# A linear state space layer and an H3 convolution on one core: finer PSUM items, a block of B by another queue, and a new order of the items

## The chip, the cores and the metric

One core of a Trainium2 chip. The metric is device microseconds of one execution of the whole program, as the median of several runs; lower is better.

## The reference

Two layers over 2,048 positions of 640 channels, side by side in the output. The first ("S5") has a diagonal complex state of 640; the second ("H3") gates a 4-tap convolution and convolves the result with a filter as long as the sequence, channel by channel.

```python
def _A_ref(x, Lambda_re, Lambda_im, B_re, B_im, C_re, C_im, log_dt, Dskip):
    Lam_bar = jnp.exp(dt * Lam)                      # 640 complex, dt = exp(log_dt)
    B_bar = ((Lam_bar - 1.0) / Lam)[:, None] * Bmat  # 640 x 640
    Bu = jnp.einsum("bld,pd->blp", x + 0j, B_bar)
    for t in range(L):
        h = Lam_bar[None, :] * h + Bu[:, t, :]
    y = 2.0 * jnp.einsum("blp,dp->bld", hseq, Cmat).real + x * Dskip

def _B_ref(q, k, v, shift_k, ssm_k, ssm_D):
    k_shift = sum of 4 shifted k, weighted by shift_k, per channel
    kv = k_shift * v
    y = causal convolution of kv with ssm_k (2,048 long), per channel, by FFT
    y = y + kv * ssm_D
    return q * y
return jnp.concatenate([a, b], axis=-1)              # 1 x 2048 x 1280, bf16
```

## The kernel before, in words

**S5.** Time is split in eight phases c, t = 8m + c, with m up to 256, so that the recurrence runs over m with the eighth power of Lam_bar. The phases of x are loaded transposed by SP's queue (`load_x`, L417, items `x0` to `x7`, two phases to a tile `xT`), and so is B (`turn_B`, L159): `B0` is the first block of 128 states, `B1` and `B3` two blocks each, and each item is one transpose for the real and one for the imaginary part. For each block j of 128 states, the PE items are `u1j` and `u3j` (B times the phases 1 and 5, 3 and 7, 512 columns for each of the real and the imaginary part, L434), `vj` (phases 2 and 6, joined with u1 by a diagonal matrix of powers of lambda, `diagL`, L449 and L450), `wj` (phase 4, joined with v and u3, 256 columns, L442) and `zj` (phase 0, joined with the seven others). Each is evicted to `u` in bf16 by an item with an e (`ue1j`, `vej`, `wej`, `zej`; L142 on ScalarE, L144 on VectorE). Then on VectorE `rsj` rotates z by a table of phases and scans it (L463 to L472), `roj` rotates back, and the states of the other phases are made from it: a product by a power of lambda (`m4j`, `m2j`, `m1j`, `m3j`; L306 on ScalarE, L308 on VectorE) and two additions (`r..`, L496). Last, sixteen items `p0` to `p15` project 128 rows each to 640 outputs, in two halves of 320 (L508). For thirteen of them the product of x and Dskip is loaded and made in rows (`xl`, `xm` L537) and added on VectorE as PSUM is read (`ye`, `dve_yx`, L523); for the other three it is five matmuls (L515) and a plain eviction. `yd` stores the rows.

**H3.** Channels go in five groups G of 128. `kT` and `vT` are loaded transposed (L561), `ks` copies k with its halves swapped, `dS` makes the diagonal matrices of the taps (L582), `tap` does the four taps on PE in 64x64 tiles (L594), `kv` multiplies by v out of PSUM (L599). `kvo` and `kvs` write kv to DRAM and read it back in another layout, `hs` loads the filter in that layout (L572), `had` adds ssm_D to it (L578). The long convolution is a two-stage transform on PE: `s1h` and `s1k` (L613), evicted to `As`; `s2` (L631), evicted to `XH`; the products `y` on VectorE (L645 to L648); the inverse `inv` (L659), evicted to `zz` (`zs`), two DMA transposes (`zt`, L667), the last stage `fin` (L681), and `ob`, which multiplies by q out of PSUM (L686). `qi` and `od` load q and store the output.

**Opening.** The tables of phases and the transform matrices are made in the kernel. Four short vectors (log_dt, Lambda_im, Lambda_re, Dskip) are loaded as rows by ScalarE's queue (`lv`, L147), PE turns them (`pv`, L247), ScalarE takes the exponent (`exp`, L250) and sine and cosine, and VectorE makes `lam` (L285), from which all powers of lambda come. `WARM` items (`wm`) are matmuls on a unit matrix ahead of S5's first products.

**Order.** `make_plan` gives each item its engine, cost, inputs and function; a planner outside of the kernel wrote the string `ORDER` from it, and the kernel issues the items in just that order, so each engine works through its items in the order of the string. `name@2` is the PSUM slot that the item uses, a trailing `v` puts an item that may run on either engine on VectorE (else ScalarE), `a` and `b` are the two buffers for the products m. PSUM is four tiles of two banks, `ps`, slots 0, 2, 4 and 6: each item of PE takes a whole tile, also `w` and `z`, which fill two half banks.

Of the kernel before, what the change touches and what calls it, by code (L numbers as in the profile page):

```python
# [46 lines left out]
class Kernel:  # L47


    def __init__(self, ctx, tc, out, ins):  # L50
# [95 lines left out]
    def load_vec(self, eng, v, ap):  # L146
        eng.dma_start(out=self.vrow[v * NT:v * NT + NT, :], in_=ap.rearrange("(j i) -> j i", i=128))  # L147

# [266 lines left out]

    def load_x(self, c):
        self.nc.sync.dma_start_transpose(  # L417
            out=self.xc(c), in_=self.x2.rearrange("(m p) (k d) -> p m k d", p=T, d=128)[c])
# [10 lines left out]
    def pe_u(self, j, c, joins, ps):  # L429
        mm = self.nc.tensor.matmul  # L430
        x = self.__dict__[f"xT{c}"]
        for r in range(2):
            for k in range(NT):
                mm(ps[:, r, :], lhsT=self.BT[:, r, k, j * 128:(j + 1) * 128], rhs=x[:, :, k, :],  # L434
                   start=(k == 0), stop=(not joins and k == NT - 1))
        self.join(j, joins, ps, lambda c2, r: self.pair(j, c2, r), 2 * M)

    def pe_w(self, j, c, joins, ps):
        mm = self.nc.tensor.matmul
        for r in range(2):  # L440
            for k in range(NT):
                mm(ps[:, r, 0:M], lhsT=self.BT[:, r, k, j * 128:(j + 1) * 128], rhs=self.xc(c)[:, k, :], start=(k == 0), stop=False)  # L442
        self.join(j, joins, ps, lambda c2, r: self.u(j, c2, int(c2 > c))[:, r, :], M)

    def join(self, j, joins, ps, src, n):
        mm = self.nc.tensor.matmul
        for r in range(2):
            for i, (s, c2) in enumerate(joins):
                mm(ps[:, r, 0:n], lhsT=self.dl(j)[:, 3 * s, :], rhs=src(c2, r), start=False, stop=False)  # L449
                mm(ps[:, r, 0:n], lhsT=self.dl(j)[:, 3 * s + 2 - r, :], rhs=src(c2, 1 - r), start=False, stop=(i == len(joins) - 1))  # L450
# [47 lines left out]
    def pe_proj(self, c, i, skip, ps):  # L498
# [3 lines left out]
        for b in range(2):  # L502
            o = ps[:, b, :]
            c0 = 320 * b
            for j in range(NT):
                h = self.u(j, c)
                for r in range(2):
                    mm(o[:, 0:320], lhsT=h[:, r, ts], rhs=self.Cs[:, r, j, c0:c0 + 320], start=(j == 0 and r == 0),  # L508
                       stop=(skip and j == NT - 1 and r == 1))
            if skip:  # L510
                continue
            pieces = [(d, max(c0, d * 128), min(c0 + 320, d * 128 + 128)) for d in range(NT)]
            pieces = [q for q in pieces if q[1] < q[2]]
            for q, (d, lo, hi) in enumerate(pieces):
                mm(o[:, lo - c0:hi - c0], lhsT=xT[:, d, ts], rhs=self.diagD[:, d, lo - d * 128:hi - d * 128],  # L515
                   start=False, stop=(q == len(pieces) - 1))

    def ev_y(self, eng, n, ps):
        out = self.yo[:, n % NYO, :].rearrange("q (b n) -> q b n", b=2)
        self.copy(eng, out, ps[:, :, 0:320])  # L520

    def dve_yx(self, n, ps):
        self.nc.vector.tensor_tensor(out=self.yo[:, n % NYO, :].rearrange("q (b n) -> q b n", b=2), in0=ps[:, :, 0:320],  # L523
                                     in1=self.xr(n).rearrange("q (b n) -> q b n", b=2), op=ALU.add)
# [168 lines left out]
def make_plan(K):  # L693
# [87 lines left out]
    for c in (1, 5, 3, 7, 2, 6, 4, 0):  # L781
        dmat(f"x{c}", 1.4, 0.3275, (), lambda c=c: K.load_x(c))
    for j in range(NT):
        bt = [f"B{(j - 1) // 2 * 2 + 1 if j else 0}"]
# [5 lines left out]
        ev(f"ve{j}", 1024, [f"v{j}", "zer"], lambda eng, ps, j=j: K.ev_u(eng, j, 2, ps), f"v{j}")  # L790
        pe(f"w{j}", 18 * P256, 36, ["x4", f"dL{j}", f"ue3{j}", f"ve{j}"] + bt, lambda ps, j=j: K.pe_w(j, 4, ((0, 3), (1, 2)), ps), f"w{j}")
        ev(f"we{j}", 512, [f"w{j}", "zer"], lambda eng, ps, j=j: K.ev_half(eng, j, 4, ps), f"w{j}")
        pe(f"z{j}", 22 * P256, 44, ["x0", f"we{j}"] + bt, lambda ps, j=j: K.pe_w(j, 0, ((0, 7), (1, 6), (2, 4)), ps), f"z{j}")
        ev(f"ze{j}", 512, [f"z{j}"], lambda eng, ps, j=j: K.ev_half(eng, j, 0, ps), f"z{j}")
# [175 lines left out]
```

## Time and profile before

| | |
|---|---|
| median of 3 runs | 197.31 us (196.41 to 197.58) |
| the profiled execution | 196.7 us |
| its span in the profile | 194.8 us, 7,192 instructions |
| PE busy | 177.1 us (91%), 3,125 matmuls |
| VectorE busy | 171.5 us (88%), 355 instructions |
| ScalarE busy | 152.4 us (78%), 207 instructions |
| GpSimd busy | 19.4 us (10%), all in the opening |
| DMA | 34.87 MB, mean 179 GB/s |
| granted clock of PE | 1.00 throughout |

The span is the time from the first to the last instruction in the profile; 1.9 us of the execution lie around it. PE is TensorE's matmuls, PEld its weight loads, DVE VectorE, ACT ScalarE, POOL GpSimd, SP the engine that issues most DMAs; a name with q at its end (SPq, ACTq) is the time that an engine took to issue a DMA. L523 is line 523 of the kernel. A row of a timeline has the start and the length in us, the engine, the line, output and inputs with their sizes, the count, and in brackets how long the engine stood idle just before and on whom it waited. A row of a group has the busy time in us and the mean of one in ns, then the idle time before. A row on a DMA ends with the median time from issue to landing in us.

### The profile page before, as it was taken

Reading aid. Unit: us, or ns where it says so; the run is one execution under the profiler, and the core shown is the slowest. Engines: PE = TensorE matmul, PEld = TensorE weight load, DVE = VectorE, ACT = ScalarE, POOL = GpSimd, SP = SyncE. Lnnn points to the kernel's source line nnn. Section 1 sums busy time; section 2 is a strip of 40 time slices with the busy share of each in tenths; the row PEclk is TensorE's granted clock in tenths of the full one; section 3 lists DMA queues with packets and bytes.
Section 4 is the critical chain, followed back from the end, with each engine's and each line's share of the span. In section 5 each row is a group of like instructions: output and inputs, shape, how many; then the busy total and the mean of one; then the engine's idle time right before and its main releaser. Section 6 shows DMA issues by size and latency. Waiting matters only on the chain. (4 is left out here: it accounts for less than half of the span.)

```text
span 194.8 us, 7192 instructions
## 1 busy us (share of the span) xinstructions
PE 177.1 (91%) x3125; PEld 122.6 (63%) x3125; DVE 171.5 (88%) x355; ACT 152.4 (78%) x207; POOL 19.4 (10%) x46
## 2 busy tenths in 40 slices
PE   7779799698989998999999896899899999999992
PEld 2233366555567757644887785677678777778771
DVE  1495966998999999999999999999899999999593
ACT  3674959696899998999999899978996799790000
POOL 8599402000000000000000000000000000000000
PEclk9999999999999999999999999999999999999999
DMA  5999999999999999799679998797730996698926
GB/s 103 169 170 191 182 151 184 270 199 175 228 168 161 196 279 189 123 182 294 111 140 168 164 283 163 136 178 175 183 112 8 216 233 136 173 204 209 274 73 207
DMA packets 133022, 34.87 MB, mean 179 GB/s; under 512 B 128512, under 2 KB 132352, under 8 KB 132992
## 3 DMA queue, kind: packets, MB, share of 16 engines
q1 hardware_dynamic: 132952, 34.42, 89.9%
q8 instruction: 24, 0.39, 0.9%
q14 instruction: 6, 0.05, 0.1%
q10 hardware_dynamic: 40, 0.01, 0.0%
HBM read 10.17 MB, written 7.86 MB: 93 GB/s over the span
## 5 line engine op out<-in xcount | busy, mean ns | idle before, releaser
L508 PE MATMUL ps<-Cs,u 128*128 128x320 bf16 x320 | 45.6, 299 | 0.9 <-DVE yo L523 0.6
L142 ACT CAST As<-ps 128x1024 bf16<-128x1024 f32 x40 | 38.9, 1033 | 3.8 <-PE ps L613 2.3
L508 PEld LDWEIGHTS <-u 128*128 128x128 bf16 x320 | 30.5, 98 | 12.9 <-issue 0.9
L142 ACT CAST XH<-ps 128x1024 bf16<-128x1024 f32 x38 | 36.0, 1029 | 2.4 <-PE ps L631 2.1
L434 PE MATMUL ps<-xT,BT 128*128 128x512 bf16 x150 | 34.4, 379 | 3.2 <-DMA xT<-in_A_x_dram 1.1
L434 PEld LDWEIGHTS <-BT 128*128 128x128 bf16 x150 | 13.9, 98 | 20.4 <-DMA xT<-in_A_x_dram 1.6
L496 DVE TENSOR_TENSOR u<-tmp,u 128x1024 bf16<-128x1024 bf16 (+1 forms) x40 | 24.5, 622 | 1.0
L142 ACT CAST u<-ps 128x1024 bf16<-128x1024 f32 (+1 forms) x20 | 16.7, 835 | 6.7 <-PE ps L434 3.4
L142 ACT CAST zz<-ps 128x1024 bf16<-128x1024 f32 x19 | 18.8, 1034 | 3.1 <-PE ps L659 3.1
L631 PE MATMUL ps<-As,Gre 64*64 64x256 bf16 x320 | 19.6, 274 | 1.5 <-DVE vT L599 0.6
L631 PE MATMUL ps<-As,nGim 64*64 64x128 bf16 x320 | 18.4, 216 | 0.4 <-issue 0.4
L631 PE MATMUL ps<-As,Gim 64*64 64x128 bf16 x320 | 18.3, 216 | 0.0
L449 PE MATMUL ps<-u,diagL 128*128 128x256 bf16 (+1 forms) x60 | 15.3, 290 | 0.0
L450 PE MATMUL ps<-u,diagL 128*128 128x256 bf16 (+1 forms) x60 | 15.3, 291 | 0.0
L599 DVE TENSOR_TENSOR vT<-ps,vT 128x1024 bf16<-128x1024 f32 x10 | 11.9, 1217 | 2.6 <-PE ps L450 1.5
L631 PEld LDWEIGHTS <-Gre 64*64 64x64 bf16 x320 | 11.1, 106 | 4.9 <-issue 3.9
L306 ACT ACTIVATE tmp<-u,lam 128x512 bf16<-128x512 bf16 (+1 forms) x18 | 13.9, 868 | 0.0
L442 PE MATMUL ps<-xT,BT 128*128 128x256 bf16 x100 | 12.6, 273 | 1.1 <-DVE vT L599 0.9
L686 DVE TENSOR_TENSOR qb<-ps,qb 128x1024 bf16<-128x1024 f32 x10 | 12.0, 1215 | 1.5 <-DMA qb<-in_B_q_dram 1.5
L646 DVE TENSOR_TENSOR XH<-XH 128x2048 bf16<-128x2048 bf16 x10 | 12.2, 1225 | 0.5
L523 DVE TENSOR_TENSOR yo<-ps,BT 128x640 bf16<-128x640 f32 x13 | 10.7, 822 | 2.2 <-PE ps L508 0.9
L308 DVE TENSOR_SCALAR tmp<-u,lam 128x512 bf16<-128x512 bf16 (+2 forms) x42 | 12.5, 359 | 0.1
(161 smaller groups left out, 305.5 us busy)
## 6 DMA issues: line engine op xcount, KB each, us to landing
h_st<-in_B_ssm_k_dram SPq DMA_DIRECT2D x10, 256.0 KB, 4.6
kv_rows<-vT SPq DMA_DIRECT2D x5, 512.0 KB, 4.6
kv_st<-kv_rows SPq DMA_DIRECT2D x10, 256.0 KB, 5.2
qb<-in_B_q_dram SPq DMA_DIRECT2D x10, 256.0 KB
out_dram<-qb SPq DMA_DIRECT2D x10, 256.0 KB, 4.4
out_dram<-yo SPq DMA_DIRECT2D x16, 160.0 KB, 2.7
BT<-in_A_x_dram SPq DMA_DIRECT2D x13, 160.0 KB, 3.1
zz<-zz SPq DMA_TRANSPOSE x10, 4.7
```

Source lines behind the costliest of these rows:

```text
L142: self.nc.scalar.copy(out=out, in_=in_)
L306: self.nc.scalar.activation(out=out, in_=in_, func=ACT.Copy, scale=w)
L308: self.nc.vector.tensor_scalar_mul(out=out, in0=in_, scalar1=w)
L434: mm(ps[:, r, :], lhsT=self.BT[:, r, k, j * 128:(j + 1) * 128], rhs=x[:, :, k, :], start=(k == 0), stop=(not joins and k == NT - 1))
L442: mm(ps[:, r, 0:M], lhsT=self.BT[:, r, k, j * 128:(j + 1) * 128], rhs=self.xc(c)[:, k, :], start=(k == 0), stop=False)
L449: mm(ps[:, r, 0:n], lhsT=self.dl(j)[:, 3 * s, :], rhs=src(c2, r), start=False, stop=False)
L450: mm(ps[:, r, 0:n], lhsT=self.dl(j)[:, 3 * s + 2 - r, :], rhs=src(c2, 1 - r), start=False, stop=(i == len(joins) - 1))
L496: v.tensor_tensor(out=o, in0=buf[:, i, 0:n], in1=o, op=ALU.add)
L508: mm(o[:, 0:320], lhsT=h[:, r, ts], rhs=self.Cs[:, r, j, c0:c0 + 320], start=(j == 0 and r == 0), stop=(skip and j == NT - 1 and r == 1))
L631: mm(out, lhsT=w[rows, k, :], rhs=rhs, start=(w is self.Gre), stop=(w is self.Gim))
L646: tt(out=X, in0=X, in1=pl(0, 1).to_broadcast([128, 8, 2, 128]), op=ALU.mult)
L686: self.nc.vector.tensor_tensor(out=q, in0=ps[:].rearrange("p b (m e) -> p b m e", e=32), in1=q, op=ALU.mult)
```

## The change

Five things, in one edit:

1. **PSUM is one tile** of eight banks, `banks`. The four `ps` of H3 are now pairs of its banks. Items whose key begins with H, all of S5's, get a single bank (slots 0 to 7).
2. **S5's items are single banks.** `u1`, `u3` and `v` become two items each, one for the real and one for the imaginary part (`u10_0`, `u10_1`), with an eviction of 512 elements each in place of one of 1,024. `w` and `z` put both parts into one bank. A projection becomes two items, one for each half of 320 columns (`p0_0`, `p0_1`), and so do its skip addition or eviction.
3. **B's first block is loaded as it lies**, 128 rows of 640, by two loads on ScalarE's queue (`load_B`) into a part of `zz` that is free at that time, turned by ten matmuls on a unit matrix (`bt0_0`, `bt0_1`) and evicted into `BT` (`bte0_0`, `bte0_1`). The other four blocks stay transposed loads.
4. **The planner's rates for DMAs** differ a little, and hold a larger cost for `hs` and `kvs`.
5. **ORDER** is new throughout. (`JV` is empty, so the new branches on it and the class c = 6 aren't used.)

Matmuls, weights and transfers are otherwise the same.

```diff
 NPS = 4
+JB = 1
+JV = ()
...
-        self.ps = [psum.tile([128, 2, 512], f32, name=f"ps{i}") for i in range(NPS)]
+        self.banks = psum.tile([128, 8, 512], f32, name="banks")
+        self.ps = [self.banks[:, 2 * i:2 * i + 2, :] for i in range(NPS)]
...
+        self.Bn = self.zz[:, 0:2 * JB * D].rearrange("p (r j d) -> p r j d", r=2, j=JB)
...
+    def load_B(self, eng, j):
+        for r, ap in enumerate((self.A_B_re, self.A_B_im)):
+            eng.dma_start(out=self.Bn[:, r, j, :], in_=ap[128 * j:128 * j + 128, :])
...
+    def pe_bt(self, js, ks, ps):
+        mm = self.nc.tensor.matmul
+        i = 0
+        for j in js:
+            for k in ks:
+                re, im = (self.Bn[:, r, j, 128 * k:128 * k + 128] for r in range(2))
+                o_re, o_im = (ps[:, r, 128 * i:128 * i + 128] for r in range(2))
+                mm(o_re, lhsT=re, rhs=self.ident[:], start=True, stop=True)
+                mm(o_im, lhsT=im, rhs=self.ident[:], start=True, stop=True)
+                i += 1
...
-    def pe_u(self, j, c, joins, ps):
+    def pe_u(self, j, c, r, joins, ps):
+        x = self.__dict__[f"xT{c}"]
+        for k in range(NT):
+            self.nc.tensor.matmul(ps, lhsT=self.BT[:, r, k, j * 128:(j + 1) * 128], rhs=x[:, :, k, :],
+                                  start=(k == 0), stop=(not joins and k == NT - 1))
+        self.join(j, r, joins, ps, lambda c2, r: self.pair(j, c2, r))
...
+    def pe_w(self, j, c, joins, ps):
+        for r in range(2):
+            o = ps[:, M * r:M * r + M]
...
-    def dve_yx(self, n, ps):
-        self.nc.vector.tensor_tensor(out=self.yo[:, n % NYO, :].rearrange("q (b n) -> q b n", b=2), in0=ps[:, :, 0:320],
-                                     in1=self.xr(n).rearrange("q (b n) -> q b n", b=2), op=ALU.add)
+    def dve_yx(self, n, b, ps):
+        s = slice(320 * b, 320 * b + 320)
+        self.nc.vector.tensor_tensor(out=self.yo[:, n % NYO, s], in0=ps[:, 0:320], in1=self.xr(n)[:, s], op=ALU.add)
...
-    for j, n in ((0, 1), (1, 2), (3, 2)):
-        dmat(f"B{j}", 2.56 if n == 1 else 2.8, 0.3275 * n, (), lambda j=j, n=n: K.turn_B(j, n))
+    dma("B0", "ACT", 0.9, 0.36, ["lv"], lambda: K.load_B(nc.scalar, 0))
+    for j in (1, 3):
+        dmat(f"B{j}", 2.8, 0.655, (), lambda j=j: K.turn_B(j, 2))
...
-x1 x5 lv pc pc2 dc gp0 wm1@0 wt wm2@2 zer dc2 pp2 pp pv@4 exp@4 x7 B0 vec@4 rho Fi rr aM trig1 wm3@6 pc3 lam dL0@v x3 tp0 tab0
+zer x5 pc lv B0 pc3 zd x7 pc2 dc wm1@0 gp0 wm3@2 wt dc2 pp pv@4 exp@4 vec@4 dD wm2@6 rho Fi gp2 bt0_0@0 rr trig1 hk tp0 tab0
+bt0_1@2 bte0_1@2v wm0@4 hp0 x3 bte0_0@0v u30_1@0 dcol u30_0@1 gp1 gp3 x1 u10_0@2 lam dL0@v u10_1@3 u10e_1@3v tp1 dL1@v B1
```

SP's list in the opening, from its first transfer to the first group's k, v and filter. `xT` are phases of x, `BT` is B, `kT` is k, `dst` and `sk_b` the small vectors of H3. Before:

```order
L417 DMA_TRANSPOSE xT_133<-in_A_x_dram 128x5x256 x2
L417 DMA_TRANSPOSE xT_135<-in_A_x_dram 128x5x256
L159 DMA_TRANSPOSE BT<-in_A_B_re_dram 128x5x128
L159 DMA_TRANSPOSE BT<-in_A_B_im_dram 128x5x128
L417 DMA_TRANSPOSE xT_135<-in_A_x_dram 128x5x256
L159 DMA_TRANSPOSE BT<-in_A_B_re_dram 128x5x256
L159 DMA_TRANSPOSE BT<-in_A_B_im_dram 128x5x256
L417 DMA_TRANSPOSE xT_134<-in_A_x_dram 128x5x256
L162 DMA sk_b<-in_B_shift_k_dram 128x5x4
```

And now:

```order
L445 DMA_TRANSPOSE xT_130<-in_A_x_dram 128x5x256
L445 DMA_TRANSPOSE xT_132<-in_A_x_dram 128x5x256 x2
L570 DMA dst<-in_B_ssm_D_dram 2x5x64 x2
L445 DMA_TRANSPOSE xT_130<-in_A_x_dram 128x5x256
L167 DMA_TRANSPOSE BT<-in_A_B_re_dram 128x5x256
L167 DMA_TRANSPOSE BT<-in_A_B_im_dram 128x5x256
L445 DMA_TRANSPOSE xT_131<-in_A_x_dram 128x5x256 x2
L445 DMA_TRANSPOSE xT_129<-in_A_x_dram 128x5x256
L584 DMA_TRANSPOSE kT<-in_B_k_dram 128x2048
```

The two transposes of 128 states are gone, the two small loads of `dst` have come forward, and x's last phase, v and the filter h follow behind `kT` in both lists.

ScalarE's list up to the exponent and the first operations behind it, with the semaphores that each row waits for. `vrow` are the short vectors, `zz` the buffer that takes B's first block. Before:

```order
L147 DMA vrow<-in_A_Dskip_dram 5x128
L154 ACT_TABLE_LOAD
L154 ACTIVATE aph_88<-hpi 128x1 [waits DVE_49]
L250 ACTIVATE dt_b<-ps_66 128x5 [waits PE_49]
L275 ACTIVATE rr<-rho 128x5 [waits DVE_49]
```

And now:

```order
L151 DMA vrow<-in_A_Dskip_dram 5x128
L155 DMA zz<-in_A_B_re_dram 128x640
L155 DMA zz<-in_A_B_im_dram 128x640 [waits DMAHW0_49]
L162 ACT_TABLE_LOAD
L162 ACTIVATE aph_85<-hpi 128x1 [waits DVE_49]
L258 ACTIVATE dt_b<-banks 128x5 [waits PE_49]
L314 ACTIVATE diagD<-ident,vec 128x128 [waits DVE_49]
L314 ACTIVATE diagD<-ident,vec 128x128 x4
L283 ACTIVATE rr<-rho 128x5 [waits DVE_49]
```

Two issues stand ahead of the table load, the second of which waits for the DMA of log_dt, and the five `diagD` now stand ahead of `rr`.

VectorE's list just ahead of the first state scan (the row on `tab` is its first operation). `h_st` is the filter, `diagS` the taps' diagonals, `Mq` a matrix of the last stage, `kS` the swapped copy of k. Before:

```order
L578 TENSOR_TENSOR h_st<-h_st,dcol_b 128x32
L582 TENSOR_TENSOR diagS<-id_70,sk_b 128x512
L241 TENSOR_SCALAR m_cv<-m_cv 128x64
L242 TENSOR_TENSOR Mq<-m_cv,m_mask 128x256
L144 CAST u_138<-ps_64 128x2x2x256
L144 COPY kS<-kT 64x1032
L463 TENSOR_TENSOR tmp<-tab_123,u_137 128x512
```

And now:

```order
L148 CAST u_134<-banks 128x2x256
L622 TENSOR_TENSOR vT<-banks,vT 128x1024
L148 CAST u_135<-banks 128x2x256
L622 TENSOR_TENSOR vT<-banks,vT 128x1024
L249 TENSOR_SCALAR m_cv<-m_cv 128x64
L250 TENSOR_TENSOR Mq<-m_cv,m_mask 128x256
L605 TENSOR_TENSOR diagS<-id_67,sk_b 128x512
L601 TENSOR_TENSOR h_st<-h_st,dcol_b 128x32
L487 TENSOR_TENSOR tmp<-tab_120,u_134 128x512
```

The filter's operation now stands right ahead of the scan; an eviction and a copy of k that stood between them are elsewhere.

More of the change, by code (lines that the diff above doesn't have):

```diff
@@ L427, in pair @@
         return self.__dict__[f"u{j}"][:, c::4, r, 2:2 + M]
-    def pe_u(self, j, c, joins, ps):
-        mm = self.nc.tensor.matmul
[L431 to L443, printed above, removed]
@@ L501, in pe_proj, with ev_y @@
         xT = self.xc(c)
[L502 to L520, printed above, removed]
-    def dve_yx(self, n, ps):
-        self.nc.vector.tensor_tensor(out=self.yo[:, n % NYO, :].rearrange("q (b n) -> q b n", b=2), in0=ps[:, :, 0:320],
-                                     in1=self.xr(n).rearrange("q (b n) -> q b n", b=2), op=ALU.add)
+        c0 = 320 * b
+        for j in range(NT):
+            h = self.u(j, c)
+            for r in range(2):
+                mm(ps[:, 0:320], lhsT=h[:, r, ts], rhs=self.Cs[:, r, j, c0:c0 + 320], start=(j == 0 and r == 0),
+                   stop=(skip and j == NT - 1 and r == 1))
+        if skip:
+            return
+        pieces = [(d, max(c0, d * 128), min(c0 + 320, d * 128 + 128)) for d in range(NT)]
+        pieces = [q for q in pieces if q[1] < q[2]]
+        for q, (d, lo, hi) in enumerate(pieces):
+            mm(ps[:, lo - c0:hi - c0], lhsT=xT[:, d, ts], rhs=self.diagD[:, d, lo - d * 128:hi - d * 128],
+               start=False, stop=(q == len(pieces) - 1))
+    def ev_y(self, eng, n, b, ps):
+        self.copy(eng, self.yo[:, n % NYO, 320 * b:320 * b + 320], ps[:, 0:320])
+    def dve_yx(self, n, b, ps):
+        s = slice(320 * b, 320 * b + 320)
+        self.nc.vector.tensor_tensor(out=self.yo[:, n % NYO, s], in0=ps[:, 0:320], in1=self.xr(n)[:, s], op=ALU.add)
     def xr(self, n):
@@ L704, in dmat @@
     def dmat(name, cost, mb, deps, fn):
-        dma(name, "SP", cost, mb, deps, fn, lat=2.1, rate=0.235)
+        dma(name, "SP", cost, mb, deps, fn, lat=2.1, rate=0.228)
     def pe(name, cost, n, deps, fn, take, mode=FULL):
@@ L790, in make_plan @@
[L790 to L794, printed above, removed]
+            pair(f"u{c}{j}", j, c, [f"x{c}", f"x{c + 4}"] + bt + [f"wm{w}" for w in range(WARM)], ())
@@ L897 @@
+p13_1@0 p12_1@1 p13_0@4 xm12 ye12_0@5 ye12_1@1 p14_0@1 xm13 yd12 ye13_0@4 ye13_1@0 yd13 ye14_0@1 yd14
 """
@@ L933 @@
                 args.append("DVE" if how.endswith("v") else "ACT")
-            tiles = [K.re["ab".index(s)] if s in "ab" else K.ps[int(s) // 2] for s in how.rstrip("v")]
-            if len(it["take"]) > 1:
-                args.append(tiles)
-            elif tiles:
-                args.append(tiles[0])
+            slot = how.rstrip("v")
+            if slot and slot in "ab":
+                args.append(K.re["ab".index(slot)])
+            elif slot:
+                key = (it["take"] or [it["give"] or it["use"]])[0]
+                tile_ = K.ps[int(slot) // 2]
+                args.append(tile_[:, int(slot) % 2, :] if key[0] == "H" else tile_)
             it["fn"](*args)
```

153 lines of the change are left out of this document (95 added, 58 removed).

## The prediction

> **What bounds the kernel now.** I read the busy shares by stage first, cut where VectorE (DVE) had its last wait of the opening and its first of the end, and cut once more at the first state scan. Columns: stretch, us, then busy us and instructions of PE, its weight loads, DVE, ScalarE (ACT) and POOL, then PE clock, DMA share, GB/s.
>
> ```profile
> 44.48:138.00 93.52, 87.33 (x1876) 63.49 (x1876) 91.11 (x164) 88.00 (x103) 0.00 (x0) 1.00 1.02 185
> 138.00:194.80 56.80, 52.01 (x1000) 39.84 (x994) 48.93 (x72) 33.36 (x40) 0.00 (x0) 1.00 0.68 170
> 0.00:36.03 36.03, 29.30 (x182) 14.07 (x183) 24.13 (x100) 22.64 (x48) 19.43 (x46) 1.00 0.96 174
> 36.03:194.80 158.77, 147.79 (x2944) 108.53 (x2944) 147.34 (x255) 129.79 (x159) 0.00 (x0) 1.00 0.90 180
> ```
>
> In the middle DVE is busy 91.11 of 93.52 us (97%), PE 87.33, ACT 88.00. Ahead of the scan at 36.03 DVE works only 24.13 us, so it stands still for 11.90. In the last stage it has 7.87 us to spare and PE 4.79. Next DVE's timeline, which says where it waits, and for whom:
>
> ```profile
> 9.04 0.23 DVE L285 TENSOR_TENSOR lam<-rr,cos 128x5 f32<-128x5 f32 x1 [1.25 <-ACT cos L138]
> 33.06 0.30 DVE L578 TENSOR_TENSOR h_st<-h_st,dcol_b 128x32 bf16<-128x32 bf16 x1 [1.56 <-DMA h_st<-in_B_ssm_k_dram]
> 36.03 0.42 DVE L463 TENSOR_TENSOR tmp<-tab,u 128x512 bf16<-128x512 bf16 x1
> 44.48 2.35 DVE L599 TENSOR_TENSOR vT<-ps,vT 128x1024 bf16<-128x1024 f32 x2 [0.92 <-DMA vT<-in_B_v_dram]
> 138.36 0.82 DVE L523 TENSOR_TENSOR yo<-ps,BT 128x640 bf16<-128x640 f32 x1 [0.49 <-DVE BT L537]
> 191.13 0.82 DVE L523 TENSOR_TENSOR yo<-ps,BT 128x640 bf16<-128x640 f32 x1 [0.46 <-PE ps L508]
> ```
>
> The last wait ahead of the scan is 1.56 us for h, an SP load. From 44.48 to 138.36 no wait is listed: DVE's own work sets the time there. PE's waits and the chain that ended last complete the picture:
>
> ```profile
> 9.19 1.04 PE L434 MATMUL ps<-xT,BT 128*128 128x512 bf16 x4 [0.94 <-DMA BT<-in_A_B_re_dram]
> 12.65 2.55 PE L434 MATMUL ps<-xT,BT 128*128 128x512 bf16 x11 [1.13 <-DMA xT<-in_A_x_dram]
> 20.33 2.32 PE L434 MATMUL ps<-xT,BT 128*128 128x512 bf16 x10 [1.01 <-DVE diagS L582]
> 35.62 0.40 PE L613 MATMUL ps<-R,h_st 64*128 64x128 bf16 x8 [1.49 <-DVE u L144]
> 45.76 1.25 PE L442 MATMUL ps<-xT,BT 128*128 128x256 bf16 x10 [0.92 <-DVE vT L599]
> 167.50 2.21 PE L681 MATMUL ps<-Mq,zz 128*64 128x64 bf16 x128 [0.25 <-DVE yo L523]
> by line: PE ps L508 9.9%; PE ps L681 2.2%; DVE yo L523 0.9%; DVE BT L537 0.2%; issue 0.1%
> ```
>
> So: the opening waits for loads, the middle is DVE's, and the end is PE's (the chain is projection L508 and inverse L681). A microsecond saved ahead of the scan is kept; one added to DVE in the middle is paid; one added to DVE in the last stage is covered by its 7.87 us; one added to PE there is paid.
>
> **The opening: SP's list loses two transposes.** SP's issues (start, us taken):
>
> ```profile
> 5.59 1.28 SPq L159 DMA_TRANSPOSE BT<-in_A_B_re_dram  x1
> 6.91 1.28 SPq L159 DMA_TRANSPOSE BT<-in_A_B_im_dram  x1
> 24.61 1.48 SPq L417 DMA_TRANSPOSE xT<-in_A_x_dram  x1
> 27.54 2.00 SPq L572 DMA_DIRECT2D h_st<-in_B_ssm_k_dram  x2
> xT<-in_A_x_dram SPq DMA_TRANSPOSE x8, 4.5
> BT<-in_A_x_dram SPq DMA_DIRECT2D x13, 160.0 KB, 3.1
> ```
>
> B0's transposes took 1.28 us of SP each; everything else ahead of h in SP's list (eight x, B1, sk, kT0, vT0, dst) is the same set in another order. So h is issued at 27.54 - 2.56 = 24.98, and with the 5.52 us that passed from issue to use (27.54 to 33.06) it is in at 30.5; its DVE operation ends at 30.8. Before, the scan came 2.67 us after that operation (33.36 to 36.03), behind a diagS, Mq, a wide eviction and a copy; in the new list the scan stands right behind it. The other input of the scan is z0: its x0 is issued at 24.61 - 2.56 = 22.05, in after the median 4.5 at 26.55, then z0's products and an eviction, under 4 us: 30.3 at most. I put the scan at 31.2, 0.4 us after h for work that is late on DVE: **-4.8 us**. Bounds: h as quick as the 160 KB loads (3.1) gives 28.8; no gain at all is 36.03.
>
> **The opening's new cost.** B0 now comes by ACT's queue, is turned on PE and evicted by DVE.
>
> ```profile
> 0.74 0.54 ACTq L147 DMA_DIRECT2D vrow<-in_A_log_dt_dram  x1
> 2.42 1.28 ACT L154 ACT_TABLE_LOAD   x1 [2.42 <-issue]
> 5.66 0.18 ACT L250 ACTIVATE dt_b<-ps 128x5 bf16<-128x5 f32 x1 [1.75 <-PE ps L247]
> L306 ACT ACTIVATE diagD<-ident,vec 128x128 bf16<-128x128 bf16 x5 | 1.6, 394 | 0.0
> ```
>
> B_im's issue waits for log_dt, issued at 0.74 and in between 3.8 (3.1 after issue) and 5.66 (its product was evicted); I take 4.4. Behind that wait on ACT stand the table load (1.28), dt_b, five diagD (5 x 0.39, now ahead of rr) and the sine chain that DVE waits for with lam: dt_b slips by about 0.75 to 6.4, the diagD end at 8.4, a second table load and three short operations follow, and lam comes at about 10.4 instead of 9.04. B_im lands at 4.4 + 3.1 = 7.5 or a little later; ten transposes and two evictions put the first product at about 10.4, where it was 9.19: +1.2 on PE. Neither is late enough to move h at 30.5, which covers them, as do DVE's 11.90 idle us. Without that cover they would cost the 1.2. A B_im that lands after about 11.6 would eat into z0's slack. The ten transposes themselves fall ahead of products that wait anyway: nothing.
>
> **DVE's work.** Groups: busy us, mean ns.
>
> ```profile
> L599 DVE TENSOR_TENSOR vT<-ps,vT 128x1024 bf16<-128x1024 f32 x10 | 11.9, 1217 | 2.6 <-PE ps L450 1.5 <-DMA vT<-in_B_v_dram 0.9
> L523 DVE TENSOR_TENSOR yo<-ps,BT 128x640 bf16<-128x640 f32 x13 | 10.7, 822 | 2.2 <-PE ps L508 0.9 <-DVE BT L537 0.7 <-ACT tmp L306 0.2
> L144 DVE CAST u<-ps 128x1024 bf16<-128x1024 f32 x4 | 4.9, 1213 | 0.0
> L144 DVE CAST u<-ps 128x512 bf16<-128x512 f32 x1 | 0.7, 683 | 0.0
> L144 DVE COPY kS<-kT 64x1032 bf16<-64x1032 bf16 x10 | 4.2, 424 | 0.3
> L144 DVE CAST zz<-ps 128x1024 bf16<-128x1024 f32 x1 | 1.2, 1225 | 0.0
> L308 DVE TENSOR_SCALAR tmp<-u,lam 128x512 bf16<-128x512 bf16 x23 | 7.2, 347 | 0.1
> L308 DVE TENSOR_SCALAR tmp<-u,lam 128x1024 bf16<-128x1024 bf16 x9 | 4.3, 479 | 0.0
> ```
>
> The skip addition: 13 of 640 become 26 of 320. From 640 and 1,024 elements, (1217 - 822)/384 = 1.03 ns an element, so 320 take 493: 26 x 0.493 - 10.7 = **+2.1** (at cost per element alone 0). S5's evictions on DVE: 4 x 1.213 + 0.683 = 5.5 become 11 x 0.683 = 7.5: **+2.0** (per element alone +1.2). B0's evictions, 1,024 and 256 wide: 1.213 + 0.42 = **+1.6**. The rest of the reordering: three kS copies and one zz eviction go to ACT, three products of L308 come (one wide, two of 512), two As come and two XH go: -1.27 - 1.22 + 0.48 + 0.69 + 0 = **-1.3**. Sum +4.4: 171.5 becomes 175.9. By the new list 23.5 of it lie ahead of the scan (24.1 before), so 152.4 behind it, +5.1. The 2.1 of the skip additions fall in the last stage, under DVE's 7.87 idle us; that leaves **+2.9** on the path (+2.1 by the lower bound). The wait of 0.92 for the second group's vT (its load moves up with the list, and two transposes of B now stand ahead of it where one of C stood) I halve: **-0.4**.
>
> ACT takes nine more instructions in all for the halves (+0.9 at most) and three copies for three products (+3.1 at most if a copy costs as much as a 1,024-wide eviction, below nothing if the products weigh more). It has 5.5 us idle in the middle and 23.4 in the last stage: nothing. If the middle's cover were gone, up to 4.
>
> **PE's changes of tile shape.** Finer items alternate between S5's 128x128 products and the other half's smaller tiles more often: by the new list 92 changes, 68 before, six of the new ones from the first projection on.
>
> ```profile
> 85.73 0.38 PE L449 MATMUL ps<-u,diagL 128*128 128x512 bf16 x1
> 85.94 0.38 PE L450 MATMUL ps<-u,diagL 128*128 128x512 bf16 x1
> 86.25 0.40 PE L613 MATMUL ps<-R,h_st 64*128 64x128 bf16 x8
> ```
>
> Starts of 512-wide products are 0.215 us apart; at the change it is 0.31: 0.09 us a change, 24 x 0.09 = 2.2 in all. In the middle PE's 6.2 idle us cover it; the six at the end are paid: **+0.5**. The Trainium skill, "TensorEngine Tiling (Array Packing)", section Key Properties, says that a change of tiling mode drains the engine; "TensorE: Matmul & The Clock Gate", section Single matmul latency, puts the drain at about 175 ns. By that page's figure, as an estimate, the six would cost 1.1 and the 24 4.2; the rows show half of it, and I go by the rows.
>
> **The tail.** The last skip addition is 0.493 instead of 0.82: **-0.3**. The single PSUM tile I cost at nothing: addresses and number of banks are the same, and the new list's waits are still between an item and its own bank's.
>
> **Sum:** -4.8 - 0.4 + 2.9 + 0.5 - 0.3 = -2.1. The profiled execution took 196.7 with a span of 194.8; it becomes 192.7 and 194.6. It lay 0.6 under the median of 197.3, so the median becomes **195.2**, 1.1% faster. About 1%, 2 us, is what a measurement of this kernel can tell from no change.
>
> **Rivals.**
> *PE becomes the bound.* Once DVE starts 4.8 us earlier, PE's list may be the longer one: first product +1.2, changes of shape +2.2, the four stalls (1.13 + 1.01 + 1.49 + 0.92 = 4.55) halved by earlier loads -2.3, tail -0.3: +0.8, a median of 198.1. For it: PE has only 0.25 us of waits after 167 and 93% in the middle, and the end is its own already. Against it: it needs the 6.2 idle us of the middle to be no cover.
>
> *The DMA engines pace the opening (slower).* Their share is 0.96 up to the scan, so an SP that issues earlier may only lengthen the queue. The loads then land when they did, the four stalls of PE stay, and first product, changes of shape and tail make +1.2 + 2.2 - 0.3 = +3.1: 200.4. It decides once the stalls shrink by less than 1.1 us (3.1 - 1.1 = 2.0, the 1%). For it: the share, and B0's bytes are as many as before. Against it: DVE's own part of the gain (the 2.67 us behind h) needs no faster load, and the waits of PE name DVE three times out of four. The Trainium skill, "DMA: Bandwidth & Descriptors", section Issuing engines are not separate DMA queues, takes this side: transfers issued by several engines run on the same 16 DMA engines, and only the sequencer's issuing time is saved. Here that issuing time is 1.28 us a transpose, which is not small.
>
> *The one tile couples its banks.* If waits went by tile, each of 199 PE items would wait for the eviction before it, at 0.68 us some 135 us more, over 330 in all. The new list's waits show no sign of it.
>
> **Chances.** Forecast 0.44, PE as the bound 0.35 (within 1%), DMA-paced 0.20 and coupled banks 0.01 (slower). The forecast's own range goes from 191.5 (scan at 28.8, -2.4; evictions at cost per element, -0.8; free changes, -0.5) up to 197. The whole range goes on to 200.4, the DMA rival's price; about a tenth lies above it and less below 191.5.
>
> **What would show it.** Right: first product near 10.4, lam near 10.4, h's DVE operation near 30.5 and the scan near 31.2; DVE near 176 us in all with no wait over 0.5 from there to about 135; skip additions near 493 ns; PE with few waits in the end. Wrong: h's operation still near 33 with a DMA wait (the queue paces); long DVE waits for PE in the middle (PE is the bound); skip additions near 411 or over 550 ns; a first product after 11.6.

## The result and the profile after

The changed kernel takes 195.0 us in the median (194.15 to 195.83, four runs) against 197.4 for the kernel before: a ratio of 0.989, with an interval of 0.985 to 0.993. Some executions of any of these kernels fall into a slower state, and ratios and intervals, here and below, leave them out. The profiled execution took 195.0 with a span of 192.7, where the prediction had 194.6 and 192.7. The sum came out; its terms did not all come out, and the experiments moved the cause of the gain to another place than the one I had named first.

The busy times by stage of the changed kernel, cut at its first scan (columns as before):

```profile
0.00:33.02 33.02, 28.22 (x160) 13.86 (x160) 24.19 (x102) 23.23 (x51) 19.98 (x46) 0.90 1.01 171
33.02:192.70 159.68, 151.36 (x2977) 107.74 (x2975) 150.78 (x275) 130.95 (x170) 0.00 (x0) 1.00 0.93 183
138.00:192.70 54.70, 50.82 (x989) 38.26 (x987) 48.31 (x82) 29.85 (x36) 0.00 (x0) 0.99 0.68 169
```

VectorE stands still for 8.83 us ahead of the scan (11.90 before) and 8.90 behind it (11.43 before); its work grew from 171.5 to 175.0. So the span's -2.1 is -3.1 of idle time ahead of the scan, -2.5 behind it, and +3.5 of work. Its timeline, where it waits and around the scan:

```profile
6.70 0.18 DVE L262 COPY vec<-banks 128x20 f32<-128x20 f32 x1 [4.36 <-ACT dt_b L258]
9.86 1.56 DVE L148 CAST BT<-banks 128x256 bf16<-128x256 f32 x2 [1.01 <-PE banks L432]
11.33 0.16 DVE L293 TENSOR_TENSOR lam<-rr,cos 128x5 f32<-128x5 f32 x1
23.86 0.80 DVE L148 COPY kS<-kT 64x1032 bf16<-64x1032 bf16 x1 [0.65 <-DMA kT<-in_B_k_dram]
...
31.88 1.10 DVE L605 TENSOR_TENSOR diagS<-id,sk_b 128x512 bf16<-128x512 bf16 x1
32.90 0.29 DVE L601 TENSOR_TENSOR h_st<-h_st,dcol_b 128x32 bf16<-128x32 bf16 x1
33.02 0.42 DVE L487 TENSOR_TENSOR tmp<-tab,u 128x512 bf16<-128x512 bf16 x1
43.62 2.35 DVE L622 TENSOR_TENSOR vT<-banks,vT 128x1024 bf16<-128x1024 f32 x2
...
182.47 2.36 DVE L709 TENSOR_TENSOR qb<-banks,qb 128x1024 bf16<-128x1024 f32 x2 [1.50 <-PE banks L704]
```

Between 23.86 and 180 no wait of 0.2 us or more is listed on VectorE: neither h nor vT is waited for any longer. h's operation came at 32.90 behind a diagS and without a wait, so what held the scan was VectorE's own list, from its wait for kT at 23.86 on. h itself was in at 32.1, by the rows on its two loads (length of an issue, first and last start, then the time from the last issue to landing):

```profile
L595 SPq DMA_DIRECT2D h_st<-in_B_ssm_k_dram x2: 710/1511/2312, 25.7 to 26.4; - x2
DMA to landing us min/median/max: 5.7/5.7/5.7
```

Before, the second of them was issued at 28.4 and landed 4.6 later, at 33.0. So h was issued 1.9 us earlier and came in 0.9 earlier. PE's waits of the opening, the one near the end, and the groups that the sum was made of:

```profile
6.29 0.17 PE L255 MATMUL banks<-ident,vrow 20*128 20x20 bf16 x1 [1.50 <-DMA vrow<-in_A_Dskip_dram]
8.68 0.29 PE L432 MATMUL banks<-ident,zz 128*128 128x128 bf16 x1 [1.20 <-DMA zz<-in_A_B_im_dram]
11.47 10.31 PE L460 MATMUL banks<-xT,BT 128*128 128x512 bf16 x40
29.18 0.72 PE L468 MATMUL banks<-xT,BT 128*128 128x256 bf16 x5 [0.55 <-DMA xT<-in_A_x_dram]
187.89 1.52 PE L532 MATMUL banks<-Cs,u 128*128 128x320 bf16 x10 [0.27 <-DVE yo L547]
```

```profile
L547 DVE TENSOR_TENSOR yo<-banks,BT 128x320 bf16<-128x320 f32 x26 | 11.8, 486 | 0.7 <-PE banks L532 0.2 <-DVE BT L560 0.2
L148 DVE CAST u<-banks 128x512 bf16<-128x512 f32 x11 | 7.4, 686 | 0.9 <-PE banks L460 0.5 <-ACT Gre L142 0.4
L622 DVE TENSOR_TENSOR vT<-banks,vT 128x1024 bf16<-128x1024 f32 x10 | 12.1, 1221 | 0.1
```

The halves cost what their rows promised singly (486 ns, estimated 493; 686 ns, estimated 683), but 26 additions of 486 ns fill only 11.8 us, since those that follow one another overlap (five in a row, from 177.40 on, take 2.08 us): +1.1 where I had +2.1. SP's list, last, which carries the opening:

```profile
0.73 6.03 SPq L445 DMA_TRANSPOSE xT<-in_A_x_dram  x3
18.66 2.54 SPq L584 DMA_TRANSPOSE kT<-in_B_k_dram  x1
25.65 3.07 SPq L595 DMA_DIRECT2D h_st<-in_B_ssm_k_dram  x2
```

Three transposes of x took 6.03 us to issue (4.81 before), and h was issued at 25.65, 1.9 earlier than before and not 2.6.

### The profile page after: what moved, and what is told of

It is laid out like the page before. It is cut to its first block, busy times and chain, and to the rows that moved or that the text cites. A ratio compares the mean times of both kernels' runs of the same rounds, so it can differ in the third digit from the quotient of the medians.

```text
span 192.7 us, 7254 instructions
## 1 busy us (share of the span) xinstructions
PE 179.6 (93%) x3135; PEld 121.6 (63%) x3135; DVE 175.0 (91%) x375; ACT 154.2 (80%) x220; POOL 20.0 (10%) x46
## 5 line engine op out<-in xcount | busy, mean ns | idle before, releaser
L532 PE MATMUL banks<-Cs,u 128*128 128x320 bf16 x320 | 46.2, 299 | 0.3 <-DVE yo L547 0.3
L146 ACT CAST XH<-banks 128x1024 bf16<-128x1024 f32 x40 | 39.1, 1032 | 5.3 <-PE banks L654 5.3
L146 ACT CAST As<-banks 128x1024 bf16<-128x1024 f32 x38 | 37.6, 1043 | 0.8 <-PE banks L636 0.8
L460 PE MATMUL banks<-xT,BT 128*128 128x512 bf16 x150 | 37.4, 392 | 0.6 <-DVE u L148 0.6
L146 ACT CAST u<-banks 128x512 bf16<-128x512 f32 x29 | 16.8, 594 | 6.0 <-PE banks L460 3.5
L146 ACT CAST zz<-banks 128x1024 bf16<-128x1024 f32 x20 | 20.2, 1035 | 1.6 <-PE banks L682 1.6
L654 PE MATMUL banks<-As,Gre 64*64 64x256 bf16 x320 | 19.4, 274 | 1.2 <-DVE As L148 0.8
L654 PE MATMUL banks<-As,Gim 64*64 64x128 bf16 x320 | 18.0, 216 | 0.0
L654 PE MATMUL banks<-As,nGim 64*64 64x128 bf16 x320 | 18.0, 216 | 0.0
L475 PE MATMUL banks<-u,diagL 128*128 128x256 bf16 (+1 forms) x60 | 15.9, 291 | 0.0
L474 PE MATMUL banks<-u,diagL 128*128 128x256 bf16 (+1 forms) x60 | 15.9, 290 | 0.0
L547 DVE TENSOR_TENSOR yo<-banks,BT 128x320 bf16<-128x320 f32 x26 | 11.8, 486 | 0.7 <-PE banks L532 0.2
```

What stands on the lines that cost most here:

```text
L146: self.nc.scalar.copy(out=out, in_=in_)
L460: self.nc.tensor.matmul(ps, lhsT=self.BT[:, r, k, j * 128:(j + 1) * 128], rhs=x[:, :, k, :], start=(k == 0), stop=(not joins and k == NT - 1))
L474: mm(o, lhsT=self.dl(j)[:, 3 * s, :], rhs=src(c2, r), start=False, stop=False)
L475: mm(o, lhsT=self.dl(j)[:, 3 * s + 2 - r, :], rhs=src(c2, 1 - r), start=False, stop=(i == len(joins) - 1))
L532: mm(ps[:, 0:320], lhsT=h[:, r, ts], rhs=self.Cs[:, r, j, c0:c0 + 320], start=(j == 0 and r == 0), stop=(skip and j == NT - 1 and r == 1))
L654: mm(out, lhsT=w[rows, k, :], rhs=rhs, start=(w is self.Gre), stop=(w is self.Gim))
```

## The experiments

All ratios are to the kernel before, measured beside it on the same chip; a difference to the changed kernel is taken between the ratios (0.01 is 2.0 us), with about 1 us of uncertainty where nothing else is said.

| kernel | ratio | interval | first scan |
|---|---|---|---|
| the change | 0.989 | 0.985 to 0.993 | 33.0 |
| change, B0 by SP | 0.992 | 0.988 to 0.997 | 34.4 |
| before, B0 by ScalarE | 1.002 | 0.997 to 1.006 | 37.7 |
| before, finer items | 1.001 | 0.996 to 1.006 | 35.8 |
| before, scan right behind z0 | 0.998 | 0.995 to 1.002 | 34.2 |
| change, four PSUM tiles | 1.139 | 1.130 to 1.149 | 37.5 |
| change, clock held | 0.988 | 0.977 to 0.998 | 32.6 |
| change, clock held and lam ahead of B0 | 0.990 | 0.986 to 0.994 | 31.5 |
| change, +2.4 us VectorE in the middle | 0.996 | 0.993 to 1.000 | 33.7 |
| change, +2.1 us ScalarE in the middle | 0.987 | 0.980 to 0.995 | 33.1 |
| change, +2.6 us PE in the middle | 0.993 | 0.989 to 0.997 | 32.6 |
| change, +2.4 to 2.9 us VectorE at the end | 1.005 | 1.002 to 1.008 | 31.8 |
| change, +2.8 us PE at the end | 1.004 | 1.001 to 1.007 | 32.2 |

**B0 undone, and B0 alone.** In the changed kernel, B0 goes back to SP's queue:

```diff
-    dma("B0", "ACT", 0.9, 0.36, ["lv"], lambda: K.load_B(nc.scalar, 0))
-    for j in (1, 3):
-        dmat(f"B{j}", 2.8, 0.655, (), lambda j=j: K.turn_B(j, 2))
+    for j, n in ((0, 1), (1, 2), (3, 2)):
+        dmat(f"B{j}", 2.8, 0.3275 * n, (), lambda j=j, n=n: K.turn_B(j, n))
...
-zer x5 pc lv B0 pc3 zd x7 ... wm0@4 hp0 x3 bte0_0@0v u30_1@0
+zer x5 pc lv pc3 zd x7 ... wm0@4 hp0 x3 B0 u30_1@0
```

> The changed kernel with only B's first block put back: two transposes on SP behind the third x, no turning on PE, no evictions of it on VectorE. Theory O (the gain comes from SP's list being shorter in the opening): h is issued 2.6 us later, its VectorE operation moves to about 35.5, and the time goes back to 196.5 to 197.5. Theory L (the gain comes from the finer items and the new list, and the scan of the changed kernel is set by VectorE's own work since it has no wait from 24 us on): VectorE loses 1.6 us of work and a wait of 1.0 ahead of the scan, h at 33.3 is at most 0.5 later, and the time stays within 0.7 us of 195.0.

0.992: 0.7 us slower than the change, plus or minus 1.2. That is theory L's time, but the interval reaches into theory O's; h was issued at 27.56, 1.9 later than in the change, and the scan came 1.4 later, more than the 0.5 of theory L. In the kernel before, the same loads, turns and evictions are put in:

```diff
-... exp@4 x7 B0 vec@4 rho Fi rr aM trig1 wm3@6
+x1 x5 lv B0 ... exp@4 x7 vec@4 rho Fi bt0_0@0 rr aM trig1 bt0_1@2 bte0_1@2v bte0_0@0v wm3@6
```

> The kernel before with only B's first block changed: loaded as it lies by ScalarE's queue, turned on PE, evicted by VectorE; list and items otherwise those of before. Theory O: h is issued 2.6 us earlier and in near 30.5, the scan follows 3.0 us behind it at 33.4 instead of 36.0, and the time falls by 2 to 2.6, to about 195.0. Theory L: the loads are in no earlier because the transfers' engines are full (share 0.96), or the products start later by as much; scan within 1 us of 36, time 196.5 to 198.

1.002: no gain (0.4 us longer, plus or minus 0.9). Theory O falls here. SP's list in this kernel, PE's waits and VectorE's:

```profile
0.73 9.07 SPq L442 DMA_TRANSPOSE xT<-in_A_x_dram  x4
27.26 3.09 SPq L597 DMA_DIRECT2D h_st<-in_B_ssm_k_dram  x2
```

```profile
9.73 0.29 PE L429 MATMUL ps<-ident,zz 128*128 128x128 bf16 x1 [2.95 <-DMA zz<-in_A_B_im_dram]
10.66 3.64 PE L419 MATMUL ps<-ident 128*128 128x512 bf16 x8
14.14 2.11 PE L459 MATMUL ps<-xT,BT 128*128 128x512 bf16 x9
```

```profile
33.63 0.30 DVE L603 TENSOR_TENSOR h_st<-h_st,dcol_b 128x32 bf16<-128x32 bf16 x1 [0.37 <-DMA h_st<-in_B_ssm_k_dram]
37.74 0.42 DVE L488 TENSOR_TENSOR tmp<-tab,u 128x512 bf16<-128x512 bf16 x1 [0.74 <-ACT u L143]
```

The two transposes are gone from SP's list, but its four issues of x take 9.07 us, where before three took 4.81 and the fourth 1.41: 2.85 more, as much as was saved. h is issued at 27.26 instead of 27.54, and VectorE, which waits for it, gets it at 33.63 instead of 33.06. That is the DMA rival's mechanism, in this list. The part of B is in at 9.7, the first product starts at 14.1 instead of 9.2, and the scan is 1.7 later. Part of PE's delay comes from where I put the turning: eight matmuls of the `WARM` items stand between it and the first product, and take 3.64 us. Another place for it was not tried.

**The finer items alone.** The kernel before with PSUM as one tile and every item of S5 cut in its halves, one behind the other at the old item's place:

```diff
-u10@2 u30@4 ... ue10@2v ... p0@2 ... ye0@2
+u10_0@2 u10_1@3 u30_0@4 u30_1@5 ... u10e_0@2v u10e_1@3v ... p0_0@2 p0_1@3 ... ye0_0@2 ye0_1@3
```

> The kernel before with S5's items cut into single banks and PSUM as one tile, in the list of before: each old item stands as its two halves one behind the other, each old eviction as two, on the same engine; B's first block by SP as before. Theory F (finer items alone bring the gain, since a half is released earlier): 194.5 to 196. Theory N (the gain needs the list that was made for them): the halves only cost, up to 1.1 us of VectorE for the skip additions, 0.6 for its evictions and 1.6 of ScalarE, time 197.5 to 199.5.

1.001, scan at 35.8: theory N. The halves neither cost nor bring anything that can be measured in the old list. From here to the change with B0 by SP, which differs in the list alone (0.992), it is -1.7 us, plus or minus 1.3.

**PSUM as four tiles again.**

```diff
-        self.banks = psum.tile([128, 8, 512], f32, name="banks")
-        self.ps = [self.banks[:, 2 * i:2 * i + 2, :] for i in range(NPS)]
+        self.ps = [psum.tile([128, 2, 512], f32, name=f"ps{i}") for i in range(NPS)]
```

> The changed kernel with PSUM as four tiles of two banks again, single banks taken as halves of these; items, list and addresses the same. If the one tile costs or brings nothing: 195.0 within 0.5 us. If the one tile couples its banks: faster by over 1 us. If two items in the halves of one small tile are coupled by it: slower by over 1 us.

1.139: 30 us longer than the change, in the direction of the third expectation and far beyond it. Addresses, items and list are the same; the waits that the program carries are not. One instance, in the rows of VectorE, ScalarE and PE in turn:

```profile
87.26 0.69 DVE L147 CAST u<-ps 128x512 bf16<-128x512 f32 x1
```

```profile
87.99 0.59 ACT L145 CAST u<-ps 128x512 bf16<-128x512 f32 x1 [4.94 <-DVE u L147]
```

```profile
88.62 1.23 PE L467 MATMUL ps<-xT,BT 128*128 128x256 bf16 x5 [4.35 <-ACT u L145]
```

An eviction of one half on ScalarE waits 4.94 us until VectorE has read the other half of the same tile, and PE waits 4.35 us for ScalarE. Two evictions by different engines, of two banks of one small tile, are put one behind the other; in the tile of eight banks they are not. The rival on coupled banks had the thing upside down: the one tile is what uncouples them, and the new list would be worth nothing without it. Why a large tile is followed by its parts and a small one isn't was not looked into.

**The clock.** Two groups of four matmuls on the unit matrix more:

```diff
-... pp pv@4 exp@4 ... bt0_0@0 rr trig1
+... pp wm4@6 pv@4 exp@4 ... wm5@2 bt0_0@0 rr trig1
```

> The changed kernel with two more groups of four matmuls on the unit matrix, one ahead of the turning of the short vectors and one ahead of the turning of B. In the changed kernel PE waited 1.5 and 1.2 us there and its granted clock was 0.5 from about 9.6 to 14.4. If that clock costs time: first products at full speed, S5's first evictions about 2 us earlier, the scan 1 to 2 us earlier, time 193 to 194.2. If VectorE's work or the x loads set the opening: clock 1.0, but PE only waits for x instead, and time 194.5 to 195.3.

0.988: no difference that can be seen, though the interval is wide. In the changed kernel's trace the clock (the third number from the end) had been this, from 7.0 on:

```profile
7.00:9.60 2.60, 1.40 (x12) 1.02 (x11) 1.61 (x10) 2.58 (x7) 1.46 (x6) 0.64 1.03 189
9.60:12.00 2.40, 2.40 (x9) 0.72 (x7) 2.14 (x11) 2.30 (x9) 2.29 (x4) 0.50 0.89 188
12.00:14.40 2.40, 2.40 (x7) 0.78 (x6) 2.36 (x10) 0.00 (x0) 2.32 (x3) 0.50 1.16 209
14.40:17.00 2.60, 2.60 (x13) 1.23 (x12) 2.57 (x11) 1.63 (x3) 1.37 (x3) 0.97 1.01 77
```

The column alone misleads, since it can show 1.00 where PE runs at about half its speed. The same group of four matmuls on the unit matrix, just ahead of the first products, tells the speed; here with PE's work doubled at the end, and then with VectorE's (both kernels stand below):

```profile
9.29 1.88 PE L423 MATMUL banks<-ident 128*128 128x512 bf16 x4
8.95 1.03 PE L423 MATMUL banks<-ident 128*128 128x512 bf16 x4
```

The column has 1.00 for both. Six kernels share the changed kernel's opening: the change itself and the five below that make something twice, counted up to the scan. In five of them the group took 1.9 us, with scans at 32.2 to 33.7; in one it took 1.03, with the scan at 31.8. With the clock held it took 1.03 too, and the scan still came at 32.6. So full speed alone did not bring the scan forward. The six scans, and those of the two versions with the clock held, follow SP's issue of kT instead: it went out between 17.4 and 18.7, and the scan came 14.1 to 15.0 us behind it, in nearly the same order. VectorE's last listed wait ahead of the scan was for kT or sk in all six. That is an order seen in the traces and was not tested by an edit.

**Work made twice.** To see which engine sets the middle and the end, the change with some items issued twice, the second time over the same values:

```diff
+REP = {"s1ke0_1": 2, "s1ke1_0": 2}
...
-            it["fn"](*args)
+            for _ in range(REP.get(n, 1)):
+                it["fn"](*args)
```

The other four take `s1ke0_0` and `s1ke1_1` (ScalarE), `u32_0` and `v2_0` (PE), six of `ye8` to `ye10` (VectorE, end), `p9_0` and `p10_1` (PE, end).

> The changed kernel with two of VectorE's evictions of As (first and second group) made twice, the second time over the same values: 2 x 1.22 = 2.4 us more of VectorE, nothing else. If VectorE's own work sets the middle: 2.0 to 2.6 longer, 197.0 to 197.6. If PE sets it: under 1 longer.

+1.4 us for 2.4 of work, plus or minus 1.0: more than half of it, less than the expectation; the interval (0.4 to 2.4) excludes neither VectorE as the bound nor the rival, which allows up to 1.

> The changed kernel with two of ScalarE's evictions of As in the same places made twice: 2 x 1.04 = 2.1 us more of ScalarE. If ScalarE's idle time covers it, as I costed its part: under 0.5 longer. If all three engines are tied (90 of 94 us busy in the middle): 1.5 to 2.5 longer.

-0.3 for 2.1 of work, plus or minus 1.7: covered, as I had costed it; the interval doesn't rule out a part.

> The changed kernel with two items of S5's third block (u3 and v, real part) made twice on PE: 12 products of 512 columns at 0.215 = 2.6 us more of PE. Forecast's view (VectorE sets the middle, PE's idle 4 us there cover it): under 0.8 longer. Rival (PE is the bound): 2.0 to 2.8 longer.

+0.8 for 2.6 of work: nearer to cover than to PE as the bound, and its interval (-0.3 to 1.9) stays just under the rival's price.

> The changed kernel with six of the last skip additions made twice: 6 x 0.41 to 0.49 = 2.4 to 2.9 us more of VectorE, all in the last 20 us. If the end is PE's and VectorE has room there, as I took it for the halves of the skip additions: under 0.6 longer. If not: 2 to 2.9 longer.

+3.1, the full price. This one went against my forecast. PE's rows at the end of this kernel say why:

```profile
179.35 1.52 PE L533 MATMUL banks<-Cs,u 128*128 128x320 bf16 x10 [1.34 <-DVE yo L548]
182.13 1.52 PE L533 MATMUL banks<-Cs,u 128*128 128x320 bf16 x10 [1.25 <-DVE yo L548]
```

PE has to wait 1.34 and 1.25 us for banks that VectorE has not read yet. In the changed kernel's trace there is one such wait, of 0.27.

> The changed kernel with two of the last projection halves made twice on PE: 20 products of 320 columns at about 0.14 = 2.8 us more of PE in the last 25 us. If PE sets the end: 2.2 to 2.9 longer. If the end is set elsewhere: under 1 longer.

+3.0: PE sets the end, as expected. There, PE and VectorE are two sides of one chain, and the 6.4 idle us of VectorE in the last stage are not room for more work: 2.8 lie behind its last addition, 1.7 are listed as waits for PE and 0.7 as one for a load.

**An earlier scan alone.** The kernel before with one place of the list changed:

```diff
-had0 kT1 dS1 s1h0_1@2 tab2 tp4 dM H1 H0 ve1@0v ks1_1@v s1h0_0@6 ze0@4 rs0 ro0 kvo0
+had0 kT1 s1h0_1@2 tab2 tp4 H1 H0 s1h0_0@6 ze0@4 ve1@0 rs0 ro0 dS1 dM ks1_1@v kvo0
```

> The kernel before with one place of its list changed: the first scan stands right behind z0's eviction; diagS, Mq and kS's copy that stood between h's operation and the scan come behind it, and v1's eviction goes to ScalarE (1.21 us less of VectorE). Loads and PE's list as before. If an earlier scan is what the new list gives: scan at 34.2 to 34.6 instead of 36.0 and the time 1.0 to 2.5 less, 195 to 196.4. If the loads or PE's list behind it set the time: scan as early, time within 0.8 of before.

An eviction of 1.2 us went from VectorE to ScalarE with it. The scan came at 34.2, 1.8 us earlier, and the ratio is 0.998: -0.3 us, plus or minus 0.7. The rows by stage:

```profile
0.00:34.22 34.22, 28.17 (x173) 13.59 (x174) 21.80 (x96) 22.66 (x49) 19.57 (x46) 1.00 0.91 171
34.22:138.00 103.78, 96.95 (x1974) 69.17 (x1974) 100.99 (x189) 97.89 (x122) 0.00 (x0) 1.00 1.02 189
138.00:194.20 56.20, 51.61 (x980) 39.43 (x978) 48.19 (x71) 32.68 (x39) 0.00 (x0) 1.00 0.68 168
```

Ahead of the scan VectorE has 2.3 us less work than before (21.80, 24.13), behind it 1.8 more (149.18, 147.34); its idle time ahead of it is 12.4 us, 0.5 more than before. What stood between h and the scan was work that has to be done anyway. A scan that comes earlier because work went behind it brought nothing that can be measured here (1.0 us at most by the interval).

**A version that does more.** The change with the clock held, B0's evictions on ScalarE and the diagD behind the sine chain:

```diff
-vec@4 dD wm2@6 ... hk tp0 tab0 bt0_1@2 bte0_1@2v wm0@4 hp0 x3 bte0_0@0v u30_1@0
+vec@4 wm2@6 ... hk tp0 bt0_1@2 bte0_1@2 wm0@4 hp0 x3 bte0_0@0 tab0 dD u30_1@0
```

> The changed kernel with the two groups of matmuls that hold the clock, the two evictions of B's first block on ScalarE instead of VectorE, and the five diagD behind the sine chain, so that lam no longer waits for B: lam at about 9 instead of 11.3, VectorE 1.6 us less work. If VectorE sets the opening too: scan at 30.5 to 31.5, time 193 to 194. If the loads now set it (kT and sk waited for at 23 and 25): scan not before 32, time 194.3 to 195.3.

The scan came at 31.5, as in the first expectation, and the time is that of the second: the ratio is 0.990, the same as the change's (0.2 us apart, plus or minus 1.1). Its profiled execution was the shortest of all, 193.4 with a span of 191.1, but seven runs reach to 195.5; nothing measurable is gained.

## Why the prediction was right, and where it was not

**The total** (195.2, measured 195.0) is right because two errors of 1.7 to 1.8 us took each other out, and that is luck. In VectorE's account the forecast was -4.8 for the scan, +5.1 of work behind it and -2.3 of idle time there (the covered 2.1, with -0.4, +0.5 and -0.3); measured were -3.0, +3.4 and -2.5.

**The scan's -4.8** was mis-sized: -3.0 in the profiled execution (between -2.3 and -4.2 in the six executions of this opening, against one trace of the kernel before). Two steps of that term failed. "So h is issued at 24.98", and in at 30.5, took SP's issue times and the loads' own time for fixed. The first three transposes of x took 4.7 to 5.0 us to issue in the four kernels with B0 on SP's queue, and 5.5 to 6.6 in the nine of the new list that load B0 by ScalarE's beside them; h was issued at 25.65 here (25.1 to 27.3 in the five others) and was in at 32.1. In the old list the longer issues ate nearly the whole 2.6 us. And the scan "0.4 us after h for work that is late on DVE" took h for the load that matters. In the new list kT and sk stand later (issued at 18.66 and 21.25, before at 16.85 and 14.83), VectorE's last wait is for one of them, and from its end its list ran 7.3 to 9.2 us to the scan in the six executions. Here it came to h's operation at 32.90, 0.8 after h was in, so an h at 30.5 would not by itself have brought the scan to 31.2. The 2.67 us of work behind h that I counted as gained is, by the experiment with the earlier scan, no gain that can be measured; it had to be done ahead of h or behind the scan.

**VectorE's work behind the scan**, +5.1, was +3.4: the skip additions cost 1.1 instead of 2.1 in busy time, and 0.7 more than I had thought was done ahead of the scan (24.19, estimated 23.5). The reordering's terms hold: 175.0 in all, estimated 175.9.

**"The 2.1 of the skip additions fall in the last stage, under DVE's 7.87 idle us"** is wrong as a reason. The doubled additions at the end cost their full price. In the changed kernel's trace PE found its banks read in time (one wait of 0.27 us), so the halves did not hold it there; that VectorE had 7.87 us to spare is not the reason, and whether their 1.1 us cost anything is not shown.

**The wait for vT**, -0.4, was -0.9: it is gone. **The first product** came at 11.47 instead of 10.4: the issue of B's imaginary part did not wait until 4.4 but began at 2.78, and PE had it only at 8.68, where I had taken 3.1 us for the load. **lam** came at 11.33 instead of 10.4, since its VectorE operations stand behind B0's evictions, which PE released at 9.86. As I had it, neither moved the sum, as far as can be measured: the version with lam at 9.7 is as fast.

**The end** is PE's, as said (+3.0 for 2.8). From PE's last product to the end of the span it is 3.3 us, 3.7 before: the tail's -0.3 holds. The +0.5 for changes of tile shape was not measured by itself. **The middle** looks more like VectorE's than PE's, +1.4 of 2.4 against +0.8 of 2.6, but the intervals overlap; ScalarE's work cost nothing that can be seen. PE as the bound is not borne out; that one engine alone sets the middle isn't shown either.

**The single tile**, costed at nothing, adds no wait, as said; that the new list cannot do without it, by 30 us, was not foreseen.

**Where the gain comes from.** By the ratios, finer items in the old list give +0.2 us, the new list -1.7 (plus or minus 1.3), B0 by ScalarE's queue -0.7 (plus or minus 1.2) in the new list and +0.4 in the old one, with its turning where I put it there. The larger part is thus the list, by these ratios, and not the two transposes that I put first, though their interval reaches -1.8 us. The list is written in the finer items and needs the single PSUM tile. VectorE's 5.6 us less idle time, spread over opening (-3.1), vT and the rest (-2.5), against 3.5 more work, is where the change shows. Which places in it bring the 2.5 behind the scan was not settled, nor whether B0's part is more than nothing.

## What to carry to other kernels

Where one engine is busy nearly throughout, count its idle time over the whole span: an earlier milestone that is bought by moving work behind it brought nothing here, and idle time that it spends waiting for a partner at the end is not room for more work. A queue's issue time is not a fixed price either; move transfers to another queue and the ones that stay may take longer, so look at when the next issue starts, and which load is waited for once the list has changed. And when an item is cut into single banks, see what the evictions wait for before the cut is judged: here the same list took 225 us or 195, by how PSUM was declared.

## What the runs showed of the hardware that I had not expected

The speed of PE in the opening differed between executions of the same list of work, and the profile's clock column did not always tell it. Four 512-wide matmuls on the unit matrix took 1.9 us in five of six executions of the same opening and 1.03 in the sixth; the column has 0.50 there in three of the five, and 1.00 in the other two and in the sixth. The "1.00 throughout" of the kernel before is no better: its first eight such matmuls took 3.59 us, where ten products from 9.19 on took 2.33. The Trainium skill, "TensorE: Matmul & The Clock Gate", section What's actually happening, has the gate watch a window of about 3.4 us that runs freely, so that the same kernel can meet it differently; the traces agree in that full speed came at another time from one execution to the next.

A two-input operation of VectorE became longer while GpSimd worked: a diagS that took 0.69 us at 33.19 in the kernel before, with no GpSimd instruction beside it, took 1.10 here at 31.88, beside the second of these GpSimd rows:

```profile
30.84 0.61 POOL L367 TENSOR_TENSOR qb<-XH,Fi 128x256 int32<-128x256 int32 x1 [2.51 <-ACT tab L376]
31.53 0.90 POOL L368 TENSOR_TENSOR qb<-qb,c 128x256 int32<-128x256 int32 x1
```

It, too, was longer than its kind (0.90, where the same operation took 0.61 at 25.21). In the kernel before, a diagS at 19.50 kept its 0.69 us beside such a GpSimd operation, which took 1.14. The Trainium skill, "SBUF — State Buffer", section SBUF: two separate sides, has the two engines share a port that one of them holds for a whole instruction; the rows fit that, in that at least one of the two is longer each time, and nothing here tests it further.
